# Decays of a gated linear attention: running products by a scan, or sums of logarithms by a triangular matrix product

## The chip, the cores and the metric

The kernel runs on one core of a Trainium2 chip. The metric is the device time of one execution in microseconds (us). The engines of the core are called by the names of the profile: PE (matrix products), DVE (vector), ACT (functions and copies), POOL (general purpose; it also issues the indirect DMAs), and SP (issues the other DMAs).

## What is computed

Three stages in sequence: a gated linear attention, a mixture of experts with one expert per token, and a dense layer with `h*cos(h)`. The change is in the attention alone:

```python
f = 1.0 / (1.0 + np.exp(-f_logit))          # [4, 8, 768, 48]
for t in range(S):
    state = f[:, :, t, :, None] * state + np.einsum('bhd,bhe->bhde', k[:, :, t], v[:, :, t])
    y[:, :, t] = np.einsum('bhd,bhde->bhe', q[:, :, t], state)
```

Its output, 3072 tokens of 384 numbers, goes to the experts (each token to the one with the largest logit) and from there to the last layer.

## The kernel before

**Units.** The attention works on 24 units: 4 sequences, each of 6 chunks of 128 time steps. A unit holds all 8 heads of its chunk, as 4 pairs (`NP`): 48 numbers of head 2p on partitions 0 to 47, of head 2p+1 on partitions 64 to 111, the 128 time steps along the free dimension, so that a gate tile is 128x512. The rows between are padding.

**Gates of a unit u.** `gate_a` (ACT) takes exp(-f_logit), `gate_g` (ACT) adds one: g = 1/f. `gate_b` (DVE) runs four scans, one for each pair, that multiply g along time: r = 1/P, P being the running product of f within the chunk. `gate_ln` and `gate_exp` (ACT) give p0 = exp(-ln r), an approximate P. `gate_k` (POOL) makes k*r, `gate_q` (POOL) makes a = q*p0. `gate_d` (DVE) makes d = r*p0 and the chunk's last product `plast`, and `gate_e` (DVE) makes q = (2-d)*a, a Newton step that takes the error out of p0.

**Products of a unit.** On PE: `scores` (s, 8 products of k and q, L748), `ktrans` (kt, 4 transposes of k, L761), `y_own` (yi, the masked scores by v, L782, after a product with zeros, L777), `y_before` (y, the state of the chunk before, L792), `kvmm` (kv, k by v, L804), `xmm` (x, L830, which puts y in token order and makes the router's logits). DVE masks the scores out of PSUM (`sc`, L754) and updates the state (`S_sb`: L815 adds the product out of PSUM, L816 multiplies by `plast`). ACT copies the other results out of PSUM.

**Beside them**, from about unit 5 on, POOL scatters each unit's tokens to their experts by an indirect DMA (`xs`, L928) and splits the experts' weights in a high and a low part (`wl`, L117). SP loads units, v, weights, and clears `xs`.

**Order.** Each engine takes its instructions in program order. The class `Plan` writes that order: each step has an engine, a duration, a due time and a list of steps that it needs; `T` is the time from one unit's due times to the next one's. `keep_warm` puts small products of ones on PE where the plan has a gap there. The inputs lie in rings of five (`NIN`), and a load waits until the unit five before has given its buffer back.

Of the kernel before, what the change touches and what calls it, by code (L numbers as in the profile page):

```python
# [6 lines left out]
F32 = mybir.dt.float32  # L7
# [16 lines left out]
UB = S // CH  # L24
NP = H // 2
# [7 lines left out]
RMAX = 2.0 ** 62  # L33
F64_LO = 1.0 / 2 ** 15 * 1.125
# [606 lines left out]
def attention(tc, A, c):  # L641
    nc = tc.nc
    pe, dve, act, pool, sp = nc.tensor, nc.vector, nc.scalar, nc.gpsimd, nc.sync
    W = c["W"]
    xs, ident, ones, zeros, ctab, acc, plast = (c[n] for n in ("xs", "ident", "ones", "zeros", "ctab", "acc", "plast"))
    with ExitStack() as ctx:
        lc = ctx.enter_context(tc.tile_pool(name="lc", bufs=1))
        mask = lc.tile([128, 128], F32, name="mask")
        ucst = lc.tile([128, 128], F32, name="ucst")
        wcat = lc.tile([128, NP, 112], F32, name="wcat")  # L650
        urank = lc.tile([128, 128], BF16, name="urank")
        smask = lc.tile([128, E, GMAX], F32, name="smask")
# [3 lines left out]
        rmax = lc.tile([128, CH], F32, name="rmax")  # L656
        inp = ctx.enter_context(tc.tile_pool(name="inp", bufs=2))
        gat = ctx.enter_context(tc.tile_pool(name="gat", bufs=2))
# [9 lines left out]
        qkf = [inp.tile([128, 3, NP, CH], F32, name=f"qkf{i}", bufs=1) for i in range(NIN)]  # L668
        units, vs = {}, {}

        def load(u, apart=False):
            t = qkf[u % NIN]
            for n in ((slice(0, 1), slice(1, 3)) if apart else (slice(0, 3),)):
                for j in range(2):
                    sp.dma_start(out=t[j * 64:j * 64 + D, n], in_=A["qkf"][u, j][:, n])
            units[u] = dict(f=t[:, 0], k=t[:, 1], q=t[:, 2])
# [6 lines left out]
        st = {}  # L683
        P = Plan()
# [7 lines left out]
        def gate_a(u):  # L692
            tl = units.pop(u)
            st[u] = dict(g=gat.tile([128, NP, CH], F32, name="g"), tl=tl)
            act.activation(out=st[u]["g"], in_=tl["f"], func=AF.Exp, scale=-1.0)

        def gate_g(u):
            g = st[u]["g"]
            act.activation(out=g, in_=g, func=AF.Copy, bias=1.0)

        def gate_b(u):
            s = st[u]
            r = gat.tile([128, NP, CH], F32, name="r", bufs=3)
# [149 lines left out]
        def route(gi):  # L853
# [31 lines left out]
            ps = ps_r.tile([128, E, n], F32, name="rps", tag="ps")  # L885
# [137 lines left out]
        T = 5.8  # L1023
        for u in range(NU):
            b, ch = T * u, u % UB
            if u >= NIN:
                P.add(("ld", u), "sp", 1.65, load, (u,), b - 14, [("a", u - NIN), ("k", u - NIN)])
            if u >= 3:
                P.add(("ldv", u), "sp", 0.6, load_v, (u,), b, [("kv", u - 5), ("yi", u - 5)])
            P.add(("e", u), "act", 0.52, gate_a, (u,), b - 7.6, [("ld", u), ("b", u - 2)])  # L1030
            P.add(("g", u), "act", 0.52, gate_g, (u,), b - 7.0, [("e", u)])
            P.add(("b", u), "dve", 1.4, gate_b, (u,), b - 6.0, [("g", u), ("d", u - 3), ("k", u - 3), ("ln", u - 3)])
            P.add(("ln", u), "act", 0.52, gate_ln, (u,), b - 4.6, [("b", u), ("a", u - 2), ("d", u - 2)])
            P.add(("ex", u), "act", 0.52, gate_exp, (u,), b - 4.0, [("ln", u)])
            if u:
                P.add(("k", u), "pool", 1.23, gate_k, (u,), b - 3.5, [("b", u), ("s", u - 3), ("kt", u - 3)])
            else:
                P.add(("k", u), "dve", 0.6, gate_k, (u, dve), b - 3.5, [("b", u)])
            if u:
                P.add(("a", u), "pool", 1.23, gate_q, (u,), b - 2.4, [("ex", u), ("y", u - 3)])  # L1040
            else:
                P.add(("a", u), "dve", 0.6, gate_q, (u, dve), b - 2.4, [("ex", u)])
            P.add(("d", u), "dve", 0.8, gate_d, (u,), b - 1.8, [("ex", u), ("q", u - 2)])
            P.add(("q", u), "dve", 0.62, gate_e, (u,), b - 0.9, [("d", u), ("a", u)])
            P.add(("s", u), "pe", 1.2, scores, (u,), b, [("q", u), ("k", u), ("v0", u - 1), ("v1", u - 2)])
# [8 lines left out]
            P.add(("st", u), "dve", 0.65 if ch < UB - 1 else 0.0, state, (u,), b + T + 5.9, [("kv", u), ("y", u - 1), ("d", u)])  # L1054
# [41 lines left out]
        P.issue({("ldc", 0): 17.6} | {("ld", i): t for i, t in enumerate((4.0, 7.6, 11.0, 14.4, 16.6))}  # L1096
# [48 lines left out]
def layouts(inputs):  # L1145
    import numpy as np
    a = {}
    t = np.stack([inputs[n] for n in ("f_logit", "k", "q")]).reshape(3, B, NP, 2, UB, CH, D)
    a["qkf"] = np.ascontiguousarray(t.transpose(1, 4, 3, 6, 0, 2, 5)).reshape(NU, 2, D, 3, NP, CH)
    v = inputs["v"].reshape(B, H, UB, CH, D).transpose(0, 2, 3, 1, 4).reshape(NU, CH, DM)  # L1150
# [18 lines left out]
    a["pad"] = np.zeros((16, 3, NP, CH), np.float32)  # L1169
    a["pad"][:, 0] = 30.0  # L1170
# [16 lines left out]
_IN = ("qkf", "v", "wcat", "wgate", "cst", "pad", "itab", "ctab", "slots", "wmoe", "wffn")  # L1187
# [16 lines left out]
```

## Time and profile before

| what | value |
|---|---|
| runs of the kernel | 926.71, 928.77, 918.55 us; median 926.71 |
| the profiled execution | 921.53 us, span of its instructions 919.7 us |
| granted clock of PE, mean | 0.948 |
| PE busy over the span | 832.2 us (90%) |
| DVE busy over the span | 733.6 us (80%) |
| ACT busy over the span | 386.8 us (42%) |
| POOL busy over the span | 413.7 us (45%) |

The profiled execution lies within the runs. Shares of the whole span are a mean over the three stages; the attention has to be read by itself, and the rows below do that.

### The profile page before, as it was taken

The numbers are of one execution on the slowest core, as the hardware profiler recorded it, in microseconds if no ns is written. First come the engines' busy times: TensorE is split into PE (matmuls) and PEld (weight loads), VectorE is DVE, ScalarE is ACT, GpSimd is POOL, SyncE is SP. The second block draws the span as 40 slices with busy tenths as digits, with TensorE's granted clock in tenths as the row PEclk, the third lists the DMA queues.
The fourth block names the chain that finished last, engine by engine and source line by source line (L and its number), as shares of the span: only waits on it lengthen the run. The fifth ranks groups of instructions, "written<-read, shape, count | busy, mean of one in ns | idle before, by whom it ended". The sixth has DMA issues, their size and how long they took to land.

```text
span 919.7 us, 14462 instructions
## 1 busy us (share of the span) xinstructions
PE 832.2 (90%) x5253; PEld 740.9 (81%) x5253; DVE 733.6 (80%) x1288; ACT 386.8 (42%) x740; POOL 413.7 (45%) x369
## 2 busy tenths in 40 slices
PE   6887677789899898898899999999999999999995
PEld 5766566677788797797799898989999999999885
DVE  6999999886797796886876887778777777787990
ACT  3674566435343343353344444333333333333440
POOL 3546575643122222221225476544644554545652
PEclk7898899798899898999989999999999999999998
DMA  9995646203675855955846200000000000000001
GB/s 185 294 308 155 172 122 174 96 28 99 163 177 174 213 130 192 222 131 199 215 145 145 36 18 1 32 4 1 35 1 0 35 1 1 35 1 1 35 1 38
DMA packets 42033, 92.26 MB, mean 100 GB/s; under 512 B 12576, under 2 KB 19872, under 8 KB 41952
## 3 DMA queue, kind: packets, MB, share of 16 engines
q1 hardware_dynamic: 38880, 81.79, 34.0%
q0 software_dynamic: 3072, 9.45, 2.8%
q8 instruction: 43, 0.70, 0.3%
q14 instruction: 38, 0.31, 0.1%
HBM read 69.93 MB, written 21.29 MB: 99 GB/s over the span
## 4 chain that ended last, share of the span: by engine, by line
PE 58%; DVE 25%; DMA 9%; issue 4%; ACT 1%; POOL 1%; SPq 1%; DVEq 0%; POOLq 0%; ACTq 0%
PE ps L622 9%; PE ps L623 9%; PE ps L625 9%; PE o L374 6%; PE o L372 6%; PE o L373 6%; DMA xe<-xs 5%; DVE r L705 4%; PE o L201 3%; PE o L202 3%; PE o L203 3%; DVE S_sb L816 3%; DVE sc L754 2%; DVE a L738 2%; DVE d L731 2%
## 5 line engine op out<-in xcount | busy, mean ns | idle before, releaser
L368 POOL TENSOR_TENSOR lo<-r,hi 128x512 fp32r<-128x512 f32 (+1 forms) x96 | 148.1, 1543 | 172.4 <-ACT hi L367 91.5
L117 POOL TENSOR_TENSOR wl<-ws,wh 128x384 fp32r<-128x384 f32 x96 | 101.3, 1055 | 220.7 <-ACT wh L113 164.8
L622 PE MATMUL ps<-yh,wh 128*128 128x512 f32 (+1 forms) x480 | 189.2, 394 | 0.2 <-ACT yh L614 0.2
L623 PE MATMUL ps<-yh,wl 128*128 128x512 f32 (+1 forms) x480 | 187.3, 390 | 0.0
L625 PE MATMUL ps<-yl,wh 128*128 128x512 f32 (+1 forms) x480 | 135.0, 390 | 0.0
L367 ACT CAST hi<-r 128x512 fp32r<-128x512 f32 (+1 forms) x96 | 56.2, 586 | 168.7 <-DVE r L362 167.8
L630 DVE TENSOR_SCALAR n<-ps 128x512 f32<-128x512 f32 x96 | 66.2, 690 | 68.6 <-PE ps L625 68.6
L374 PE MATMUL o<-wh,lo 128*128 128x384 f32 x352 | 119.0, 338 | 1.3 <-POOL lo L368 1.3
L372 PE MATMUL o<-wl,hi 128*128 128x384 f32 x352 | 118.6, 337 | 0.0
L373 PE MATMUL o<-wh,hi 128*128 128x384 f32 x352 | 118.3, 336 | 0.0
L625 PEld LDWEIGHTS ps<-yl,wh 128*128 128x128 f32 x480 | 92.9, 194 | 16.1
L622 PEld LDWEIGHTS ps<-yh,wh 128*128 128x128 f32 x480 | 93.1, 194 | 11.8 <-ACT yh L614 0.3
L623 PEld LDWEIGHTS ps<-yh,wl 128*128 128x128 f32 x480 | 92.7, 193 | 11.3
L638 ACT ACTIVATE r<-r,quarter 128x512 f32<-128x512 f32 x96 | 69.6, 724 | 73.8 <-DVE r L637 73.8
L189 ACT ACTIVATE hi<-ps 128x448 fp32r<-128x448 f32 x64 | 34.9, 545 | 101.5 <-PE ps L625 98.9
L113 ACT CAST wh<-ws 128x384 fp32r<-128x384 f32 x160 | 74.8, 508 | 4.5 <-DMA ws<-in_wmoe 4.5
L637 DVE SCALAR_TENSOR_TENSOR r<-n,r 128x512 f32<-128x512 f32 x96 | 70.1, 730 | 3.3
L201 PE MATMUL o<-hi,wh 128*128 128x448 f32 x192 | 71.9, 374 | 0.0
L202 PE MATMUL o<-hi,wl 128*128 128x448 f32 x192 | 71.5, 373 | 0.0
L203 PE MATMUL o<-lo,wh 128*128 128x448 f32 x192 | 71.2, 371 | 0.0
L373 PEld LDWEIGHTS o<-wh,hi 128*128 128x128 f32 x352 | 66.1, 188 | 4.3
L372 PEld LDWEIGHTS o<-wl,hi 128*128 128x128 f32 x352 | 66.2, 188 | 3.9
(152 smaller groups left out, 1582.2 us busy)
## 6 DMA issues: line engine op xcount, KB each, us to landing
ws<-in_wmoe SPq DMA_DIRECT2D x64, 384.0 KB, 5.9
qkf<-in_qkf SPq DMA_DIRECT2D x46, 288.0 KB, 6.4
cs<-in_wffn SPq DMA_DIRECT2D x24, 512.0 KB, 6.9
wffn<-ca SPq DMA_DIRECT2D x24, 256.0 KB, 5.2
ws<-wffn SPq DMA_DIRECT2D x16, 384.0 KB, 3.9
xs<-xe SPq DMA_DIRECT2D x7, 770.0 KB, 10.2
v<-in_v SPq DMA_DIRECT2D x24, 200.0 KB, 4.8
xe<-xs SPq DMA_DIRECT2D x28, 168.4 KB, 8.4
```

Source lines behind the costliest of these rows:

```text
L113: self.nc.scalar.copy(out=h, in_=w)
L117: (eng or self.nc.gpsimd).tensor_tensor(out=l, in0=w, in1=h.bitcast(F32), op=ALU.subtract)
L201: pe.matmul(yps[e][d], wh[:, cs], hi, start=m == 0, stop=False)
L202: pe.matmul(yps[e][d], wl[:, cs], hi, start=False, stop=False)
L203: pe.matmul(yps[e][d], wh[:, cs], lo, start=False, stop=m == FT - 1)
L368: pool.tensor_tensor(out=los, in0=r[:, cs], in1=his.bitcast(F32), op=ALU.subtract)
L372: pe.matmul(o, hi, wl[:, cs], start=m == 0, stop=False)
L373: pe.matmul(o, hi, wh[:, cs], start=False, stop=False)
L374: pe.matmul(o, lo, wh[:, cs], start=False, stop=m == NF - 1)
L622: nc.tensor.matmul(out, wh[:, ws[d]], xh[:, d, :], start=d == 0, stop=False)
L623: nc.tensor.matmul(out, wl[:, ws[d]], xh[:, d, :], start=False, stop=False)
L625: nc.tensor.matmul(out, wh[:, ws[d]], xl[:, d, :], start=False, stop=d == 2)
```

## The change

The logits of f come a second time, in token order: a new input `ft`, 128 time steps on the partitions and 384 numbers along the free dimension. For each unit DVE clamps them from below (`gate_f`), ACT makes exp(-f_logit) and ln(1 + that) (`gate_e`, `gate_ln`), which is -ln f, into a tile padded to 64 columns a head (`sps`), and PE multiplies it by the triangle of ones (`gate_c`, four products of 128x128 by 128x128): the sum over the steps so far, already with head and number on the partitions and time along the free dimension. ACT then reads that PSUM tile twice, exp of it (r) and exp of its negative (p). DVE makes k = min(r, 2^62)*k in one instruction, POOL makes q = q*p, DVE copies `plast` from p. The scans, the ln and exp of r, d and the Newton step are gone, and k is no longer POOL's.

```diff
-        ps_kv = ctx.enter_context(tc.tile_pool(name="ps_kv", bufs=1, space=PSUM))
+        ps_c = ctx.enter_context(tc.tile_pool(name="ps_c", bufs=1, space=PSUM))
...
-        ps_r = ctx.enter_context(tc.tile_pool(name="ps_r", bufs=1, space=PSUM))
+        kr = ctx.enter_context(tc.tile_pool(name="ps_kr", bufs=1, space=PSUM)).tile([128, 512], F32, name="kr")
...
+        def load_f(u):
+            fs[u] = inp.tile([128, DM], F32, name="f", bufs=NIN)
+            sp.dma_start(out=fs[u], in_=A["ft"][u])
...
-            for p in range(NP):
-                dve.tensor_tensor_scan(out=r[:, p, :], data0=s["g"][:, p, :], data1=rmax, initial=1.0,
-                                       op0=ALU.mult, op1=ALU.min)
...
+        def gate_f(u):
+            dve.tensor_scalar(out=fs[u], in0=fs[u], scalar1=FMIN, scalar2=None, op0=ALU.max)
+
+        def gate_e(u):
+            st[u] = {}
+            act.activation(out=fs[u], in_=fs[u], func=AF.Exp, scale=-1.0)
+
+        def gate_ln(u):
+            act.activation(out=sps[u % 2][:, :, 0:D], in_=fs.pop(u).rearrange("t (h d) -> t h d", d=D), func=AF.Ln, bias=one)
+
+        def gate_c(u):
+            ps = st[u]["c_ps"] = ps_c.tile([128, NP, CH], F32, name="cps", tag="ps")
+            keep_warm(ps)
             for p in range(NP):
+                pe.matmul(ps[:, p, :], sps[u % 2][:, 2 * p:2 * p + 2, :].rearrange("t h d -> t (h d)"), mask,
+                          start=True, stop=True)
+
+        def gate_r(u):
...
+            act.activation(out=s["r"], in_=s["c_ps"], func=AF.Exp)
+
+        def gate_p(u):
...
+            act.activation(out=s["p"], in_=s["c_ps"], func=AF.Exp, scale=-1.0)
...
-            eng.tensor_tensor(out=s["k"], in0=s["tl"]["k"], in1=s["r"], op=ALU.mult)
+            dve.scalar_tensor_tensor(out=s["k"], in0=s["r"], scalar=RMAX, in1=kq[u % NIN][:, 0], op0=ALU.min, op1=ALU.mult)
...
-            dve.tensor_tensor(out=d, in0=s["r"], in1=s["p0"], op=ALU.mult)
-            dve.scalar_tensor_tensor(out=plast[:, u, :], in0=d[:, :, CH - 1], scalar=2.0, in1=s["p0"][:, :, CH - 1],
-                                     op0=ALU.subtract, op1=ALU.mult, reverse0=True)
...
-            dve.scalar_tensor_tensor(out=s["q"], in0=s.pop("d"), scalar=2.0, in1=s["a"],
-                                     op0=ALU.subtract, op1=ALU.mult, reverse0=True)
+        def gate_last(u):
+            dve.tensor_copy(out=plast[:, u, :], in_=st[u]["p"][:, :, CH - 1])
...
-        T = 5.8
+        T = 6.5
...
+                P.add(("ldf", u), "sp", 0.6, load_f, (u,), b - 15, [("ln", u - NIN)])
+                P.add(("ld", u), "sp", 1.2, load, (u,), b - 14, [("a", u - NIN), ("k", u - NIN)])
...
+            P.add(("f", u), "dve", 0.3, gate_f, (u,), b - 9.0, [("ldf", u)])
+            P.add(("e", u), "act", 0.5, gate_e, (u,), b - 8.4, [("f", u)])
+            P.add(("ln", u), "act", 0.5, gate_ln, (u,), b - 7.8, [("e", u), ("c", u - 2)])
+            P.add(("c", u), "pe", 1.15, gate_c, (u,), b - 7.0, [("ln", u), ("r", u - 1), ("p", u - 1)])
```

The k and q halves of a unit are loaded by two DMAs of 48 rows each as before, now without f (`kq`), and f by one DMA of 128 rows. The results of `kvmm` and of the router's counts share one PSUM tile, `kr`. The rest of the attention and all of the two later stages are the same code.

In DVE's program a unit in the middle of the attention (it multiplies the state, so it isn't the first of a sequence) stands as follows. Before, with d, a, r and g as above and `lg` the router's logits:

```order
L731 TENSOR_TENSOR d<-r,p_961 128x512
L732 SCALAR_TENSOR_TENSOR plast<-d,p_961 128x4
L705 SCALAR_TENSOR_TENSOR r<-g,rmax 128x128 x4
L754 TENSOR_TENSOR sc<-sps,mask 128x512 x2
L738 SCALAR_TENSOR_TENSOR a<-d,a 128x512
L815 TENSOR_TENSOR S_sb_95<-S_sb_94,kvps 128x192
L816 TENSOR_TENSOR S_sb_95<-S_sb_95,plast 128x192
L850 TENSOR_REDUCE lg<-xps 128x16
```

And now, with f the clamp of a unit that lies five or six units ahead of the k beside it:

```order
L700 TENSOR_SCALAR f<-f 128x384
L813 TENSOR_TENSOR S_sb_95<-S_sb_94,kr 128x192
L814 TENSOR_TENSOR S_sb_95<-S_sb_95,plast 128x192
L700 TENSOR_SCALAR f<-f 128x384
L729 SCALAR_TENSOR_TENSOR k<-r,kq_130 128x512
L752 TENSOR_TENSOR sc<-sps,mask 128x512 x2
L848 TENSOR_REDUCE lg<-xps 128x16
L737 COPY plast<-p 128x4
```

Four scans, d and the Newton step have left, k and the clamp have come; the clamp is the one row there that needs a DMA's data.

On POOL the same stretch before, with a scatter (`xs`) and the weight parts (`wl`) among the gates' products:

```order
L928 DMA xs<-x,idx 6656x385
L117 TENSOR_TENSOR wl<-ws,wh 128x384
L721 TENSOR_TENSOR k<-qkf_127,r 128x512
L117 TENSOR_TENSOR wl<-ws,wh 128x384
L928 DMA xs<-x,idx 6656x385
L844 COPY x<-itab 128x1
L726 TENSOR_TENSOR a<-qkf_127,p_1058 128x512
```

And now:

```order
L118 TENSOR_TENSOR wl<-ws,wh 128x384
L926 DMA xs<-x,idx 6656x385
L118 TENSOR_TENSOR wl<-ws,wh 128x384
L734 TENSOR_TENSOR a<-kq_134,p 128x512
L842 COPY x<-itab 128x1
L118 TENSOR_TENSOR wl<-ws,wh 128x384
L926 DMA xs<-x,idx 6656x385 x2
```

The k rows are gone, and each unit has one product less between scatters and weight parts.

## Rows read from the trace of the kernel before

**Rows 1.** Windows: length, busy PE, PEld, DVE, ACT, POOL; PEclk, DMA share, GB/s.

```profile
0.00:22.00 22.00, 14.32 (x149) 12.53 (x151) 15.03 (x30) 8.43 (x13) 9.17 (x15) 0.76 0.90 185
22.00:61.00 39.00, 34.86 (x429) 28.87 (x429) 35.81 (x85) 25.08 (x49) 17.38 (x21) 0.92 1.01 305
61.00:203.00 142.00, 105.01 (x1264) 87.15 (x1266) 134.16 (x272) 76.70 (x158) 88.94 (x88) 0.90 0.51 134
```

**Rows 2.** Scores on PE, and the experts' first product: timeline (start, us; idle before).

```profile
21.81 2.08 PE L748 MATMUL sps<-a,k 64*128 64x128 f32 x16 [2.02 <-DVE a L738]
...
61.28 1.16 PE L748 MATMUL sps<-a,k 64*128 64x128 f32 x16 [0.47 <-DVE a L738]
...
195.59 1.92 PE L748 MATMUL sps<-a,k 64*128 64x128 f32 x16 [4.51 <-DVE a L738]
...
202.82 1.16 PE L748 MATMUL sps<-a,k 64*128 64x128 f32 x16
...
221.98 0.48 PE L622 MATMUL ps<-yh,wh 128*128 128x448 f32 x1 [0.19 <-ACT yh L614]
```

**Rows 3.** DVE's groups from 61 to 203 us (busy, mean ns, idle before).

```profile
L705 DVE TENSOR_TENSOR_SCAN r<-g,rmax 128x128 f32<-128x128 f32 x60 | 32.3, 597 | 0.0
L816 DVE TENSOR_TENSOR S_sb<-S_sb,plast 128x192 f32<-128x192 f32 x11 | 21.0, 1907 | 0.4
...
L738 DVE SCALAR_TENSOR_TENSOR a<-d,a 128x512 f32<-128x512 f32 x17 | 17.2, 1014 | 1.9 <-POOL a L726 1.9
L731 DVE TENSOR_TENSOR d<-r,p 128x512 f32<-128x512 f32 x16 | 13.5, 841 | 0.0
L732 DVE SCALAR_TENSOR_TENSOR plast<-d,p 128x4 f32<-128x4 f32 x16 | 9.0, 560 | 0.6
```

**Rows 4.** Timeline of DVE: the state's product twice, k of unit 0.

```profile
6.86 0.69 DVE L721 TENSOR_TENSOR k<-qkf,r 128x512 f32<-128x512 f32 x1
...
183.67 0.36 DVE L816 TENSOR_TENSOR S_sb<-S_sb,plast 128x192 f32<-128x192 f32 x1
...
189.81 5.13 DVE L816 TENSOR_TENSOR S_sb<-S_sb,plast 128x192 f32<-128x192 f32 x1
```

**Rows 5.** Timeline of POOL beside the second of them, first and last of six rows.

```profile
188.92 1.28 POOL L928 DMA_INDIRECT xs<-x,idx  x1 [0.17 <-POOL a L726]
...
193.73 0.98 POOL L117 TENSOR_TENSOR wl<-ws,wh 128x384 fp32r<-128x384 f32 x1
```

**Rows 6.** POOL's k from 61 to 203 us, by groups.

```profile
L721 POOL TENSOR_TENSOR k<-qkf,r 128x512 f32<-128x512 f32 x16 | 22.1, 1379 | 8.9 <-issue 3.9 <-DVE r L705 3.8 <-PE ktps L761 1.1
```

**Rows 7.** Who waited for whom from 61 to 203 us: total, times, longest.

```profile
PE sps L748 <- DVE a L738: 13.9, 9, 4.5
...
PE yps L792 <- DVE S_sb L816: 11.9, 7, 6.1
```

**Rows 8.** Timeline of PE over one unit's products without a wait.

```profile
40.30 1.15 PE L830 MATMUL xps<-wcat,y 128*128 128x112 f32 x8
41.28 0.38 PE L777 MATMUL yps<-ones,zeros 128*128 128x512 bf16 x1
41.59 1.09 PE L782 MATMUL yps<-sc,v 128*64 128x128 f32 x16
42.62 1.16 PE L748 MATMUL sps<-a,k 64*128 64x128 f32 x16
43.71 1.09 PE L792 MATMUL yps<-a,S_sb 64*64 64x128 f32 x16
44.73 0.67 PE L804 MATMUL kvps<-v,kt 128*64 128x48 f32 x16
45.33 0.66 PE L761 MATMUL ktps<-ident,k 128*128 128x128 f32 x4
```

**Rows 9.** DMA issues from 20 to 60 us (KB each, median us to landing).

```profile
qkf<-in_qkf SPq DMA_DIRECT2D x16, 288.0 KB, 10.1
```

**Rows 10.** A tensor_scalar of DVE within SBUF, experts' last layer, 500 to 560 us.

```profile
L631 DVE TENSOR_SCALAR n<-n x14: 426/796/1219, 510.6 to 558.9; 128x512 f32<-128x512 f32 x14
```

More of the change, by code (lines that the diff above doesn't have):

```diff
@@ L33 @@
 RMAX = 2.0 ** 62
+FMIN = -40.0
 F64_LO = 1.0 / 2 ** 15 * 1.125
@@ L655, in attention @@
         S_sb = [lc.tile([128, NP * D + 16], F32, name=f"S_sb{i}") for i in range(2)]
-        rmax = lc.tile([128, CH], F32, name="rmax")
+        one = lc.tile([128, 1], F32, name="one")
+        sps = [lc.tile([128, H, 64], F32, name=f"soft{i}") for i in range(2)]
         inp = ctx.enter_context(tc.tile_pool(name="inp", bufs=2))
@@ L663, in attention @@
         ps_y = ctx.enter_context(tc.tile_pool(name="ps_y", bufs=1, space=PSUM))
-        ps_kv = ctx.enter_context(tc.tile_pool(name="ps_kv", bufs=1, space=PSUM))
+        ps_c = ctx.enter_context(tc.tile_pool(name="ps_c", bufs=1, space=PSUM))
         ps_x = ctx.enter_context(tc.tile_pool(name="ps_x", bufs=1, space=PSUM))
-        ps_r = ctx.enter_context(tc.tile_pool(name="ps_r", bufs=1, space=PSUM))
-        qkf = [inp.tile([128, 3, NP, CH], F32, name=f"qkf{i}", bufs=1) for i in range(NIN)]
-        units, vs = {}, {}
+        kr = ctx.enter_context(tc.tile_pool(name="ps_kr", bufs=1, space=PSUM)).tile([128, 512], F32, name="kr")
+        kq = [inp.tile([128, 2, NP, CH], F32, name=f"kq{i}", bufs=1) for i in range(NIN)]
+        fs, vs = {}, {}
         def load(u, apart=False):
-            t = qkf[u % NIN]
-            for n in ((slice(0, 1), slice(1, 3)) if apart else (slice(0, 3),)):
+            t = kq[u % NIN]
+            for n in ((slice(0, 1), slice(1, 2)) if apart else (slice(0, 2),)):
                 for j in range(2):
-                    sp.dma_start(out=t[j * 64:j * 64 + D, n], in_=A["qkf"][u, j][:, n])
-            units[u] = dict(f=t[:, 0], k=t[:, 1], q=t[:, 2])
+                    sp.dma_start(out=t[j * 64:j * 64 + D, n], in_=A["qkf"][u, j][:, 1:3][:, n])
+        def load_f(u):
+            fs[u] = inp.tile([128, DM], F32, name="f", bufs=NIN)
+            sp.dma_start(out=fs[u], in_=A["ft"][u])
         def load_v(u):
@@ new lines, in gate_ln @@
+        def gate_ln(u):
[3 more added lines that the diff above has]
+            keep_warm(ps)
+            for p in range(NP):
+                pe.matmul(ps[:, p, :], sps[u % 2][:, 2 * p:2 * p + 2, :].rearrange("t h d -> t (h d)"), mask,
+                          start=True, stop=True)
+        def gate_r(u):
+            s = st[u]
+            s["r"] = gat.tile([128, NP, CH], F32, name="r")
+            act.activation(out=s["r"], in_=s["c_ps"], func=AF.Exp)
@@ L735, in gate_e @@
-        def gate_e(u):
-            s = st[u]
-            s["q"] = s["a"]
-            dve.scalar_tensor_tensor(out=s["q"], in0=s.pop("d"), scalar=2.0, in1=s["a"],
-                                     op0=ALU.subtract, op1=ALU.mult, reverse0=True)
+            s["q"] = gat.tile([128, NP, CH], F32, name="a", bufs=3)
+            eng.tensor_tensor(out=s["q"], in0=kq[u % NIN][:, 1], in1=s["p"], op=ALU.mult)
+        def gate_last(u):
+            dve.tensor_copy(out=plast[:, u, :], in_=st[u]["p"][:, :, CH - 1])
@@ L983, in attention @@
         pool.memset(zeros, 0.0)
+        dve.memset(one, 1.0)
+        for t in sps:
+            dve.memset(t, 0.0)
         for i in range(NIN):
+            load_f(i)
+            if i == 0:
+                sp.dma_start(out=mask, in_=A["cst"][:, 128:256])
             for lo, eng in ((32, dve), (96, pool)):
                 if i < 2:
-                    eng.memset(qkf[i][lo:lo + 32, 0], 30.0)
-                    eng.memset(qkf[i][lo:lo + 32, 1:3], 0.0)
+                    eng.memset(kq[i][lo:lo + 32], 0.0)
                 else:
-                    sp.dma_start(out=qkf[i][lo + 16:lo + 32], in_=A["pad"])
+                    sp.dma_start(out=kq[i][lo + 16:lo + 32], in_=A["pad"])
             load(i, i == 0)
@@ L1031, in attention @@
[L1031 to L1045, printed above, removed]
+            P.add(("f", u), "dve", 0.3, gate_f, (u,), b - 9.0, [("ldf", u)])
@@ L1046, in attention @@
+            P.add(("a", u), "pool" if u else "dve", 1.28 if u else 0.68, gate_q, (u,) if u else (u, dve), b - 3.0,
+                  [("p", u), ("ld", u), ("y", u - 3)])
+            P.add(("pl", u), "dve", 0.1, gate_last, (u,), b - 2.0, [("p", u)])
+            P.add(("s", u), "pe", 1.2, scores, (u,), b, [("a", u), ("k", u), ("v0", u - 1), ("v1", u - 2)])
             P.add(("v0", u), "dve", 0.62, scores_evac, (u, 0), b + 1.2, [("s", u), ("y", u - 2)])
@@ L1053, in attention @@
             P.add(("kv", u), "pe", 0.6 if ch < UB - 1 else 0.0, kvmm, (u,), b + T + 5.2, [("kte", u), ("st", u - 1), ("ldv", u)])
-            P.add(("st", u), "dve", 0.65 if ch < UB - 1 else 0.0, state, (u,), b + T + 5.9, [("kv", u), ("y", u - 1), ("d", u)])
+            P.add(("st", u), "dve", 0.65 if ch < UB - 1 else 0.0, state, (u,), b + T + 5.9, [("kv", u), ("y", u - 1), ("pl", u)])
             P.add(("x", u), "pe", 1.1, xmm, (u,), b + 2 * T + 1.7, [("ye", u), ("xe", u - 1), ("lg", u - 1)])
@@ L1095, in attention @@
         keep_warm(ps_x.tile([128, NP, 112], F32, name="xps", tag="ps"), 65)
-        P.issue({("ldc", 0): 17.6} | {("ld", i): t for i, t in enumerate((4.0, 7.6, 11.0, 14.4, 16.6))}
+        P.issue({("ldc", 0): 17.6} | {("ld", i): t for i, t in enumerate((5.0, 7.6, 11.0, 14.4, 16.6))}
+                | {("ldf", i): t for i, t in enumerate((2.5, 6.0, 9.5, 13.0, 15.5))}
                 | {("ldv", i): t for i, t in enumerate((8.6, 12.2, 17.1))}, {"sp": 17.2, "pe": 6.9})
@@ L1149, in layouts @@
     a["qkf"] = np.ascontiguousarray(t.transpose(1, 4, 3, 6, 0, 2, 5)).reshape(NU, 2, D, 3, NP, CH)
+    f = inputs["f_logit"].reshape(B, H, UB, CH, D).transpose(0, 2, 3, 1, 4)
+    a["ft"] = np.ascontiguousarray(f).reshape(NU, CH, DM)
     v = inputs["v"].reshape(B, H, UB, CH, D).transpose(0, 2, 3, 1, 4).reshape(NU, CH, DM)
```

40 lines of the change are left out of this document (9 added, 31 removed).

## Prediction

> **What bounds the kernel now.** I read the windows by stage first. From 61 to 203 us, where scatters and weight splits run beside the gates, DVE is busy 134.16 of 142 us, PE 105.01, POOL 88.94, ACT 76.70 [rows 1]: DVE is full and the others wait. From 22 to 61 us the DMAs are full (share 1.01, 305 GB/s) and DVE and PE are both near 90% [rows 1]. The scores on PE give the pace. Scores 1 start at 21.81, scores 7 at 61.28, scores 23 at 202.82 us [rows 2]: 6.58 us a unit early, (202.82 - 61.28)/16 = 8.85 us later. The experts start at 221.98 us, 19.2 us after the last scores [rows 2]. That tail, and everything after it, is the same code, so the change is worth what it takes from scores 23.
>
> The table of waits names whom PE waits for later: DVE's q for the scores, 13.9 us, and the state for y, 11.9 us [rows 7].
>
> Why is DVE full? Its groups there [rows 3] are partly work and partly waiting inside the instruction. The state's product took 0.36 us at 183.67 but 5.13 us at 189.81 [rows 4]. In that stretch POOL ran six instructions without a break, from 188.92 to 194.71 us [rows 5], and DVE's instruction ended just after them. The mean of that group is 1907 ns [rows 3], so it waits 11 x (1.91 - 0.36) = 17 us. Scans, d, `plast` and the Newton step stand in the same way. Before, DVE and POOL between them have more work that excludes the other than the stretch has room for.
>
> On the wait of one DVE instruction behind POOL, the Trainium skill, page SBUF — State Buffer, section "SBUF: two separate sides", says that the two engines share a port pair as "an exclusive lock, not a bandwidth split", held for the whole instruction. The trace agrees that DVE is stopped outright, but shows more than the rule: DVE didn't get in between POOL's instructions, it waited through the rest of one and five more. By the rule alone the longest wait would be one POOL instruction, 1.28 us, the state's group would cost at most 0.36 + 1.28 = 1.64 us each, and DVE's sum below would fall by 0.2 us a unit; the forecast would stay.
>
> **The change, part by part, for the stretch from 61 to 203 us (16 units).**
>
> *DVE, removed.* The four groups scan 32.3, Newton step 17.2, d 13.5 and `plast` 9.0 us [rows 3] make 72.0 of the 134.2 us busy. Left are 62.2 us, 3.9 us a unit, the state's waits included.
>
> *DVE, added.* k costs 0.69 us where POOL was idle (unit 0) [rows 4]; the Newton step, also two inputs in SBUF, took 1.01 with its waits [rows 3]. The clamp: a tensor_scalar of 512 columns within SBUF took 426 ns at its shortest and 796 in the middle [rows 10], by 384/512 0.32 to 0.60 us. The copy of `plast` is between nothing and the 0.56 us of the old step [rows 3]. Together 1.0 to 2.2 us; I take 1.6, the middle, since POOL stays busy. DVE then needs 3.9 + 1.6 = 5.5 us a unit (4.9 to 6.1).
>
> *POOL.* k goes, 22.1 of 88.94 us [rows 1, 6]: 66.8 us, 4.2 us a unit. The runs of POOL instructions that DVE waits behind get shorter by the k in each.
>
> *ACT.* Four instructions go and four come, two of them over 384 columns in place of 512. ACT was busy 54% [rows 1]; nothing on the path.
>
> *PE, the price.* A unit without waits ran x, zero, yi, s, y and kv from 40.30 to 45.33, 5.03 us, and kt took 0.66 [rows 8]: 5.7 us. One unit in six has no y and zero (1.02 + 0.31 us) and one in six no kv (0.60) [rows 8], so the mean is 5.4. The four new products are bounded below by kt, four transposes of the same size, 0.66 us, and above by x, four f32 products of 112 columns in 0.98 us [rows 8], or 1.12 at 128 columns. They are f32 products as x is: I take 1.12, so 6.5 us a unit on PE (6.0 to 6.5). This is now the longest of the engines, where before it was DVE.
>
> *Waits that stay.* PE waited 13.9 + 11.9 = 25.8 us for DVE [rows 7], 1.6 us a unit, with DVE 94% full. With DVE at 5.5 of some 7 us I take 0.6, bounds 0 and 1.6. A unit then takes 6.5 + 0.6 = 7.1 us (6.5 to 8.1) in place of 8.85.
>
> *The early stretch.* DVE's order has the clamp of unit u as its one row that needs a DMA's data, and it stands five units ahead of k: the clamp of 14 right before k of 9 and the masks of 8. What is queued behind it is the whole of DVE, and PE behind that. By the sizes in SP's new order 17.9 MB are loaded or cleared up to f of unit 14 (15 f of 0.197 MB, 14 k and q of 0.393, ten v of 0.205, seven clears of 0.79, two weight halves of 0.39, 1.1 of pads and tables). The trace moved 22 us x 185 GB/s = 4.1 MB by 22 us and 305 GB/s after it [rows 1]: f of 14 lands at 22 + (17.9 - 4.1)/0.305 = 67 us, and scores 9 follow at about 69. By PE alone, 8 x 6.5 us after 21.81 [rows 2], they would start at 74 if scores 1 stayed where they are; they should come earlier, since the first units no longer wait for k and q before their gates start. I take 71. f as a DMA of its own adds no bytes, and landing took 10.1 us here [rows 9] with five units loaded ahead: cover enough at 6.5 us a unit.
>
> *The sum.* Scores 23 start at 71 + 14 x 7.1 = 170 us in place of 202.82: 32 us less. The ends are 69 + 14 x 6.5 = 160 (43 less) and 74 + 14 x 8.1 = 187 (15 less). Against the profiled execution, 921.53 us, that is 889 (879 to 906). The median of the runs is 5 us above it, so 894 measured from there; I say 891, between the two.
>
> **The rivals.**
>
> *A, the wait moves on.* k and the clamp each wait behind POOL as the state's product does, 1.55 us [rows 3, 4]. DVE needs 3.9 + (0.69 + 1.55) + (0.32 + 1.55) + 0.2 = 8.2 us a unit and stays the bound: 71 + 14 x 8.2 = 186, 905 us. For it: POOL keeps its scatters and weight parts, and the two new rows come after masks out of PSUM, during which POOL gets hold. Against it: POOL has a quarter less to do, and of two waiting rows in succession only the first pays. The Trainium skill, page SBUF — State Buffer, section "Who interferes with whom", has a DVE instruction with two SBUF inputs, which k is, contend with a POOL instruction that reads SBUF: it would give this rival's kind of time.
>
> *B, PE falls to its lower clock, and it gets slower.* After 4.51 us without work the scores at 195.59 took 1.92 us in place of 1.16 [rows 2], at the lower of the clock's two levels (1.2 and 2.4 GHz). The program has 95 of the products of ones that fill gaps, where it had 220. If clamps that wait for DMAs hold DVE, and PE behind it, PE's longer unit runs at half speed in a share x of the units: 6.5 x (1 + x) + 0.6 us. It decides from 71 + 14 P = 203, P = 9.4, x = 0.36; at x = 0.5 scores 23 start at 216 us: 935. Against it: PE would be busy 6.5 of 7.1 us, denser than the 105 of 142 us at which the granted clock was 0.90 [rows 1].
>
> *C, it doesn't do what it says.* The scans were only where DVE happened to wait; POOL's own run (4.2 us a unit plus its waits for scatters and for ACT) and the chain through it keep 8.85 us a unit, and only the start gains: 71 + 14 x 8.85 = 195, 8 us less, 914. Against it: d and the Newton step took 0.84 and 1.01 us on the mean [rows 3] where the like k took 0.69 without a wait [rows 4], so most of what leaves is work.
>
> *D, no waits at all.* PE's floor, scores 1 earlier too: 875 or less.
>
> **How the numbers follow.** Forecast 0.56, A 0.19, C 0.10, D 0.09, B 0.06. A measurement of this kernel, whose runs lie 1.1% apart, can't tell less than 1% from no change: 917 to 936 from the median. Faster is the forecast, A, D and 0.03 of C, which lies at the edge: 0.87; the same is the rest of C and 0.01 of B: 0.08; slower is the rest of B: 0.05. The range takes in the bounds and A: 876 to 911, and leaves out D, B and most of C.
>
> **What would show it.** Right: in the changed profile DVE falls to about 5.5 of 7 us a unit, PE is the fullest engine in the middle of the attention at a clock near 1, scores follow each other by about 7.1 us, and the last start near 170 us; the four new products take 1.12 us together. Wrong: the state's product and k at 1.5 us and more on the mean (A), a granted clock below 0.85 there (B), the old step of 8.85 us (C), or DVE standing idle before the clamp with a DMA as the releaser for more than some 4 us in total, in which case scores 9 come well after 74 us.

## The result, and the profile after

The changed kernel takes 896.7 us (median of four runs, 892.5 to 899.3) where the kernel before took 926.6 beside it: ratio 0.969 (0.962 to 0.976), 30 us less. The forecast was 891 us, from 876 to 911. The profiled execution after took 899.3 us with a span of 897.4, so that of after is the slowest of its four, while that of before lies 5 us under its median: from profile to profile only 22 us can be found.

The windows by stage of the changed kernel (columns as in [rows 1]; 174 is where scores 23 start, 196.8 the experts):

```profile
0.00:22.00 22.00, 16.67 (x190) 15.29 (x191) 9.33 (x21) 9.82 (x17) 5.16 (x11) 0.92 0.82 192
22.00:61.00 39.00, 35.82 (x425) 29.78 (x426) 20.54 (x62) 22.16 (x46) 10.08 (x16) 0.96 1.00 317
61.00:174.00 113.00, 106.35 (x1282) 88.97 (x1280) 74.95 (x193) 72.38 (x151) 61.79 (x70) 0.95 0.60 165
174.00:196.80 22.80, 19.50 (x178) 16.46 (x178) 12.09 (x69) 10.15 (x23) 4.89 (x9) 0.85 0.20 66
196.80:897.40 700.60, 662.19 (x3253) 597.99 (x3253) 539.86 (x849) 269.41 (x506) 294.54 (x238) 0.97 0.30 79
```

The third row answers to the third of [rows 1]: 113 us in place of 142, and PE, not DVE, is the busy engine, 106 of 113 us (DVE 75) at a granted clock of 0.95. The timeline of PE at six places, first product of the experts last (answers to [rows 2]):

```profile
73.85 1.16 PE L746 MATMUL sps<-a,k 64*128 64x128 f32 x16 [0.49 <-POOL a L734]
...
84.17 2.08 PE L746 MATMUL sps<-a,k 64*128 64x128 f32 x16 [3.48 <-POOL a L734]
...
92.43 1.16 PE L713 MATMUL cps<-mask,soft 128*128 128x128 f32 x8
93.52 1.16 PE L746 MATMUL sps<-a,k 64*128 64x128 f32 x16
...
173.87 1.16 PE L746 MATMUL sps<-a,k 64*128 64x128 f32 x16
...
196.81 0.47 PE L623 MATMUL ps<-yh,wh 128*128 128x448 f32 x1 [0.19 <-ACT yh L615]
```

Scores 9 start at 73.85 and scores 23 at 173.87: (173.87 - 73.85)/14 = 7.14 us a unit. Before, scores 9 stood here (timeline of PE):

```profile
78.84 1.16 PE L748 MATMUL sps<-a,k 64*128 64x128 f32 x16
```

By the same two scores it was 8.86 us a unit. The triangle's products c hold PE for 1.09 us, from 92.43 to 93.52. From scores 23 to the experts it is 22.9 us, where it was 19.2 [rows 2]. DVE's groups from 61 to 174 us (answer to [rows 3]):

```profile
L729 DVE SCALAR_TENSOR_TENSOR k<-r,kq 128x512 f32<-128x512 f32 x16 | 19.0, 1187 | 11.9 <-ACT r L719 10.8 <-DMA ws<-in_wmoe 0.9
L737 DVE COPY plast<-p 128x4 f32<-128x4 f32 x16 | 7.5, 469 | 0.0
L814 DVE TENSOR_TENSOR S_sb<-S_sb,plast 128x192 f32<-128x192 f32 x10 | 4.8, 484 | 0.3
L700 DVE TENSOR_SCALAR f<-f 128x384 f32<-128x384 f32 x11 | 3.9, 353 | 4.5 <-DMA f<-in_ft 4.5
```

Here the state's product is L814: 484 ns in place of 1907. Most of its waiting is gone in this profile; in two later ones of the same kernel (runs 5 and 9 below) it took 617 and 908 ns.

Whom does PE still wait for? The row of PE at 84.17 says POOL's a, 3.48 us, and the scores after it run at the lower clock (2.08 us in place of 1.16). The timeline of POOL just before:

```profile
75.31 1.04 POOL L926 DMA_INDIRECT xs<-x,idx  x1 [0.43 <-DMA xs<-x,idx]
81.46 1.36 POOL L926 DMA_INDIRECT xs<-x,idx  x1 [5.11 <-DMA xs<-x,idx]
82.85 1.27 POOL L734 TENSOR_TENSOR a<-kq,p 128x512 f32<-128x512 f32 x1
```

Two scatters stand in a row in POOL's queue. The second waits for the first to land, 5.11 us without any work, and a, for which the scores wait, stands behind both. This is the kind of row on which the experiments turn.

### The profile page after: what moved, and what is told of

The parts are those of the page before. It is cut to its first block, busy times and chain, and to the rows that moved or that the text cites. A ratio compares the mean times of both kernels' runs of the same rounds, so it can differ in the third digit from the quotient of the medians.

```text
span 897.4 us, 14522 instructions
## 1 busy us (share of the span) xinstructions
PE 840.5 (94%) x5320; PEld 748.5 (83%) x5320; DVE 656.8 (73%) x1191; ACT 383.9 (43%) x740; POOL 376.5 (42%) x344
## 4 chain that ended last, share of the span: by engine, by line
PE 67%; DMA 13%; DVE 9%; issue 4%; POOL 1%; ACT 1%; SPq 1%; POOLq 0%; DVEq 0%; ACTq 0%
PE ps L623 9%; PE ps L624 9%; PE ps L626 9%; PE o L375 7%; PE o L373 6%; PE o L374 6%; DMA xe<-xs 5%; DMA ws<-in_wmoe 4%; PE o L202 3%; PE o L203 3%; PE o L204 3%; PE sps L746 2%; DMA xs<-x,idx 2%; PE xps L828 2%; PE yps L780 2%
```

## The experiments

The theory at the start was the prediction's: DVE was the bound, PE is it now. The rival was C: the scans hid little, and POOL's queue set the pace. Ratios are to the kernel before, run beside each. Runs 1 to 4, 5 to 8 and 9 to 12 shared a chip each, so versions of different groups are best compared by ratio. The expectations call PE TensorE, DVE VectorE, ACT ScalarE and POOL GpSimd. The table puts all profiles side by side; all columns but the last are from the timeline of PE, "the rest" is the span's end less the experts' start.

| kernel | scores 9, us | scores 23, us | us a unit between | to the experts, us | the rest, us | median, us |
|---|---|---|---|---|---|---|
| before | 78.84 | 202.82 | 8.86 | 19.2 | 697.7 | 926.6 |
| changed | 73.85 | 173.87 | 7.14 | 22.9 | 700.6 | 896.7 |
| 1 old, k on DVE | 75.38 | 195.44 | 8.58 | 15.9 | 704.9 | 915.5 |
| 2 old, no scan | 73.40 | 197.71 | 8.88 | 20.0 | 706.0 | 923.8 |
| 3 old, bare | 72.66 | 187.03 | 8.17 | 18.0 | 704.4 | 909.5 |
| 4 changed, c twice | 76.68 | 180.34 | 7.40 | 19.5 | 705.5 | 905.2 |
| 5 changed again | 70.84 | 168.90 | 7.00 | 21.6 | 702.8 | 896.2 |
| 6 scatters apart | 70.54 | 163.81 | 6.66 | 32.3 | 701.2 | 900.9 |
| 7 c in halves | 72.39 | 165.70 | 6.67 | 25.1 | 705.1 | 898.7 |
| 8 changed, k on POOL | 72.40 | 176.88 | 7.46 | 22.6 | 704.3 | 906.2 |
| 9 changed, third time | 73.31 | 174.78 | 7.25 | 22.7 | 703.2 | 899.1 |
| 10 apart early only | 72.75 | 164.70 | 6.57 | 21.4 | 702.9 | 891.4 |
| 11 old, bare, k on DVE | 73.13 | 175.69 | 7.33 | 20.2 | 699.9 | 904.5 |
| 12 changed, a on DVE | 72.14 | 167.30 | 6.80 | 22.3 | 706.5 | 898.5 |

**1. One part alone: k leaves POOL.**

```diff
-P.add(("k", u), "pool", 1.23, gate_k, (u,), b - 3.5, ...
+P.add(("k", u), "dve", 0.7, gate_k, (u, dve), b - 3.5, ...
```

> The kernel before, with one thing of the change alone: k goes from GpSimd to VectorE (same tensor_tensor). Theory (VectorE was full between 61 and 203 us, 134 of 142 us, by work and by waiting behind GpSimd): 16 k of 0.69 us add 11 us there, and the 22 us that leave GpSimd take at most about as much waiting off; so no gain: 920 to 945 us, ratio 0.99 to 1.02. Rival (GpSimd's own run of k, a, scatters and weight parts set the pace, and k leaving it is what the change gained): 8.85 us a unit falls by up to 1.38, some 15 to 22 us faster, 905 to 912.

Measured: 915.5 us, ratio 0.984 (0.979 to 0.990): 14 us faster, nearly the rival. DVE got 16 more instructions and stayed full (115 of the 120 us between scores 9 and 23), yet its state's product, 1907 ns in [rows 3], lost its waits (DVE's groups of this kernel, 61 to 187 us):

```profile
L705 DVE TENSOR_TENSOR_SCAN r<-g,rmax 128x128 f32<-128x128 f32 x62 | 29.6, 538 | 0.0
...
L816 DVE TENSOR_TENSOR S_sb<-S_sb,plast 128x192 f32<-128x192 f32 x10 | 3.6, 358 | 0.3
```

**2. One part alone: the scans' work goes.**

```diff
-for p in range(NP):
-    dve.tensor_tensor_scan(out=r[:, p, :], data0=s["g"][:, p, :], data1=rmax, ...)
+dve.tensor_scalar(out=r, in0=s["g"], scalar1=RMAX, scalar2=None, op0=ALU.min)
```

> The kernel before, with the four scans of a unit replaced by one min over the same 512 columns: the running product is left out (r is the single step's factor), and the overflow guard is set so that it can't fire; all else, the Newton step and k on GpSimd too, is as before. Theory: VectorE loses 32.3 us less 16 passes of about 0.6, 23 us of the 134 between 61 and 203 us, and nothing is added to TensorE, so about 1.4 us a unit: 8.85 becomes 7.4, 895 to 908 us. Rival C (the scans hid nothing): within 1% of before, 917 to 936.

Measured: 923.8 us, ratio 0.993 (0.990 to 0.997). The theory fell here. The windows of this kernel (61 us to scores 23) have DVE at 110 of 137 us, nobody full, and PE's granted clock at 0.85, where it was 0.90:

```profile
61.00:198.00 137.00, 105.30 (x1226) 89.80 (x1231) 109.77 (x222) 74.15 (x152) 81.45 (x86) 0.85 0.52 137
```

and the pace is what it was, 8.88 us a unit. The timeline of POOL, then DVE, then PE of the same kernel at one long unit, a row or two of each, shows why:

```profile
130.49 1.01 POOL L926 DMA_INDIRECT xs<-x,idx  x1 [2.64 <-DMA xs<-x,idx]
131.54 1.27 POOL L724 TENSOR_TENSOR a<-qkf,p 128x512 f32<-128x512 f32 x1
...
132.84 1.74 DVE L736 SCALAR_TENSOR_TENSOR a<-d,a 128x512 f32<-128x512 f32 x1 [3.26 <-POOL a L724]
...
134.64 2.08 PE L746 MATMUL sps<-a,k 64*128 64x128 f32 x16 [2.94 <-DVE a L736]
```

A scatter waits on POOL, a behind it, the Newton step on DVE behind a, the scores on PE behind that. DVE stood idle before its Newton step for 12.9 us, waiting for POOL's a, where it was 1.9 before [rows 3] (DVE's groups of this kernel, 61 to 198 us):

```profile
L736 DVE SCALAR_TENSOR_TENSOR a<-d,a 128x512 f32<-128x512 f32 x16 | 13.5, 845 | 12.9 <-POOL a L724 12.9
```

Part of the time taken off DVE became waiting for POOL.

**3. The removal without its price.**

```diff
-dve.tensor_tensor(out=d, in0=s["r"], in1=s["p0"], op=ALU.mult)
-dve.scalar_tensor_tensor(out=plast[:, u, :], in0=d[:, :, CH - 1], ...)
+dve.tensor_copy(out=plast[:, u, :], in_=s["p0"][:, :, CH - 1])
...
-dve.scalar_tensor_tensor(out=s["q"], in0=s.pop("d"), ...)
```

and the scans replaced as in 2.

> The kernel before without scans (one min in their place), without d and without the Newton step (the last column of p is copied instead): running product and correction are left out, no product with the triangle is put in, k stays on GpSimd; the overflow guard is set so that it can't fire. This is the change's removal without its price. Theory: VectorE loses some 54 of 134 us, TensorE needs 5.4 us a unit and 0.6 of waits, so 6.0 to 6.4 us a unit after 61 us: scores 23 at 157 to 165, 875 to 885 us, that is 12 to 20 us less than the changed kernel, which pays 1.1 us a unit on TensorE for the four products. Rival (GpSimd, which keeps k, is what bounds once the scans are gone): 7 us a unit or more, 893 to 905, no better than the changed kernel.

Measured: 909.5 us, ratio 0.976 (0.971 to 0.982). With nothing added to PE it is not 12 to 20 us faster than the changed kernel but some 6 to 11 slower (ratio 0.976 against 0.965 to 0.970), and slower than the rival's 905 too. Its table of waits (61 to 187 us) names POOL's k:

```profile
PE ktps L754 <- POOL k L719: 11.7, 5, 3.5
```

**4. PE's price doubled.**

```diff
-for p in range(NP):
+for p in list(range(NP)) * 2:
     pe.matmul(ps[:, p, :], sps[u % 2][:, 2 * p:2 * p + 2, :]..., mask, start=True, stop=True)
```

> The changed kernel with the four products of the triangle made twice into the same place (the second overwrites the first). Theory (TensorE is the bound now, 106.4 of 113 us busy): all of it shows, 24 x 1.09 = 26 us, 16 to 26 as far as the early units wait for DMAs: 913 to 923 us. Rival A (VectorE behind GpSimd's lock still sets the pace): TensorE has room, less than 8 us: under 905.

Measured: 905.2 us, ratio 0.972 (0.966 to 0.978), against 896 to 899 and 0.965 to 0.970 for the changed kernel: 6 to 9 of the 26 us by the medians, 2 to 7 by the ratios. That is far from the theory and at the rival's edge. PE is now full, at a clock of 1.00 (windows, 61 us to scores 23), of the long units three late ones of 8.3 to 9.2 us are left, and a full unit takes 7.6 us:

```profile
61.00:180.00 119.00, 116.79 (x1412) 100.33 (x1413) 77.88 (x190) 73.50 (x153) 62.66 (x70) 1.00 0.53 155
```

So the changed kernel's PE has some 0.5 us a unit in it, of waiting and of work at a lower clock (0.95 there), which the second c used up first.

**Revised theory.** PE's own work, near 6.6 us a unit, is one bound; the other is POOL's queue, in which scatters that wait hold a (and before the change k too) back. Run 5 is the changed kernel itself.

> The changed kernel once more, unaltered, beside the next three on the same chip, so that they can be compared with it to less than a per cent: 892 to 902 us.

Measured: 896.2 us, ratio 0.965 (0.960 to 0.969).

**6. The scatters apart.**

```diff
-done[name] = free["sp"] + self.AFTER
+done[name] = free["sp"] + self.AFTER + 2.5
```

> The changed kernel with one constant of the planner altered: a scatter counts as landed 2.5 us later than it did. It changes no instruction, only the order: where GpSimd had two scatters in a row and a behind them, a now stands between them. Theory (revised after the first four runs: GpSimd's queue stands at the second scatter until the first has landed, 3 to 5 us, and a, for which the scores wait, stands behind it; four units of the changed kernel take 8 to 10 us in place of 6.7 for that): these long units vanish, 4 x 2 to 3 us, so 6.6 to 6.9 us a unit in place of 7.14 and 5 to 12 us less in all, 885 to 892. Rival (the long units are TensorE's lower clock or late loads of f): within 3 us of the changed kernel.

Measured: the pace fell as the theory said, to 6.66 us a unit, and scores 23 came 5 us before those of run 5. But the whole took 900.9 us, ratio 0.968 (0.964 to 0.973), 5 us more than run 5 and outside both ranges. The timeline of POOL at the end shows who gave it back:

```profile
175.17 0.98 POOL L926 DMA_INDIRECT xs<-x,idx  x1 [0.45 <-POOL x L842]
...
179.86 0.96 POOL L926 DMA_INDIRECT xs<-x,idx  x1 [0.57 <-POOL idx L905]
183.27 0.96 POOL L926 DMA_INDIRECT xs<-x,idx  x1 [2.45 <-DMA xs<-x,idx]
191.54 0.96 POOL L926 DMA_INDIRECT xs<-x,idx  x1 [7.31 <-DMA xe<-xs]
```

Scatters that had been put off are left over after the last a, at least 3.4 us apart, and the load of the first expert's rows waits for the one at 183.27 (the one at 191.54 in turn for that load): 32.3 us from scores 23 to the experts.

**7. c from fp32r halves.**

```diff
-act.activation(out=sps[u % 2][:, :, 0:D], in_=fs.pop(u)..., func=AF.Ln, bias=one)
+act.activation(out=fs[u], in_=fs[u], func=AF.Ln, bias=one)
+act.copy(out=sph[u % 2][:, :, 0:D], in_=fs[u]...)
+dve.tensor_tensor(out=spl[u % 2][:, :, 0:D], in0=fs.pop(u)..., in1=sph[u % 2]..., op=ALU.subtract)
-pe.matmul(ps[:, p, :], sps..., mask, start=True, stop=True)
+for t in (sph, spl):
+    pe.matmul(ps[:, p, :], t[u % 2]..., maskr, start=t is sph, stop=t is spl)
-T = 6.5
+T = 6.0
```

> The changed kernel with the softplus split into a rounded high part (one more copy on ScalarE) and the rest (one more subtraction on VectorE), both in the fp32r type in which the experts' products run, so that a unit has four products with the high and four with the low part in place of four f32 products that count as eight; the planner's step is 6.0 in place of 6.5. First theory (TensorE is the bound): c falls from 1.09 to about 0.55 us, 0.54 x 24 = 13 us less, 882 to 888. Revised theory (part of TensorE's time is waiting for GpSimd's a anyway; the doubled c cost 0.46 of its 1.09 us a unit): 3 to 8 us less, 888 to 894. Rival (fp32r products of 128 columns are no faster than f32 ones): 8 or more products of the same length, no gain, or slower by VectorE's extra 0.4 us a unit: 896 to 910.

Measured: 898.7 us, ratio 0.966 (0.962 to 0.970), the rival. The timeline of PE has eight products in 1.04 us, up to the 85.27 of the next row:

```profile
84.23 0.33 PE L722 MATMUL cps<-maskr,softh 128*128 128x128 f32 x1
84.40 0.27 PE L722 MATMUL cps<-maskr,softl 128*128 128x128 f32 x1
...
85.07 0.27 PE L722 MATMUL cps<-maskr,softl 128*128 128x128 f32 x1
85.27 0.67 PE L811 MATMUL kr<-v,kt 128*64 128x48 f32 x16
```

c is hardly shorter, so its pace of 6.67 us has probably come from the other order that goes with the step of 6.0; no run tried that order alone.

**8. k back on POOL.**

```diff
-dve.scalar_tensor_tensor(out=s["k"], in0=s["r"], scalar=RMAX, in1=kq[u % NIN][:, 0], ...)
+(pool if u else dve).tensor_tensor(out=s["k"], in0=kq[u % NIN][:, 0], in1=s["r"], op=ALU.mult)
```

> The changed kernel with k back on GpSimd (a plain product: the cap of r is left out). Theory of the prediction (work taken off VectorE was the gain, GpSimd has room at 4.2 + 1.4 = 5.6 us a unit): VectorE is relieved of 0.7 to 1.2 us a unit, TensorE stays the bound, 7.1 to 7.4 us a unit, within 5 us of the changed kernel, up to 902. Rival, as the run without scans and correction suggests (TensorE waited 24 us for GpSimd's k there, at 8.1 us a unit): 8.1 us a unit or more, 15 to 25 us slower, 910 to 922.

Measured: 906.2 us, ratio 0.975 (0.970 to 0.980) against run 5's 0.965: 10 us slower, 7.46 us a unit, between the two. PE's waits for POOL's a (61 us to scores 23) are 6.9 us where run 5 had 2.5, none is for k.

> The changed kernel again, unaltered, beside the next three on the same chip: 893 to 900 us.

Measured: 899.1 us, ratio 0.970 (0.966 to 0.973).

**10. Apart, but not at the end.**

```diff
-done[name] = free["sp"] + self.AFTER
+done[name] = free["sp"] + self.AFTER + 2.5 * (name[1] < 12)
```

> The changed kernel with the planner's 2.5 us on a scatter's landing for the first 12 units alone; from unit 12 on the constant is the old one. With it for all units, scores followed each other by 6.66 us, scores 23 came 5 us earlier, but the last four scatters stood in a row at the end, each waiting for the one before to land, and the experts started 32.3 us after scores 23 in place of 21.6. Theory: the pace stays 6.6 to 6.8 us a unit and the tail goes back to 21 to 24 us: experts at 186 to 189, 3 to 7 us less than the changed kernel. Rival (the scatters need the time wherever they stand, so that what the pace gains the end gives back): within 2 us of it.

Measured: 891.4 us, ratio 0.960 (0.957 to 0.963), clear of run 9 beside it: 7.7 us less, the fastest version here. The experts start at 186.11. The timeline of POOL now has an a between the scatters:

```profile
75.84 1.02 POOL L926 DMA_INDIRECT xs<-x,idx  x1 [0.46 <-DMA ws<-in_wmoe]
...
80.72 1.27 POOL L734 TENSOR_TENSOR a<-kq,p 128x512 f32<-128x512 f32 x1 [0.43 <-ACT p L724]
82.15 1.28 POOL L926 DMA_INDIRECT xs<-x,idx  x1 [0.16 <-issue]
```

and the windows have PE at 101.3 of 104 us, at a clock of 1.00, with no wait for a left in the table:

```profile
61.00:165.00 104.00, 101.27 (x1274) 84.88 (x1274) 73.37 (x194) 71.28 (x151) 63.10 (x70) 1.00 0.63 178
```

**11. The removal without its price, k on DVE too** (the edits of 1 and 3 together).

> The kernel before without scans (one min in their place), without d and the Newton step, and now with k on VectorE too: GpSimd carries what it carries in the changed kernel, VectorE about the same, and TensorE has no products with the triangle. The running product and the correction are left out, and the overflow guard is set so that it can't fire. Theory (the gain is k off GpSimd and work off VectorE together, the price is c on TensorE): TensorE needs 5.6 us a unit, and with the scatters in GpSimd's queue as they are some 0.5 to 1 us of waits: 6.1 to 6.6 after the loads are in, 880 to 890 us, 6 to 16 less than the changed kernel. Rival (the queue of scatters on GpSimd bounds at about 7.1 whatever TensorE does, c is hidden): within 5 us of the changed kernel, 891 to 901.

Measured: 904.5 us, ratio 0.977 (0.972 to 0.981): by ratio no faster than run 3, slower than the changed kernel by 5 us, and outside both ranges, though PE has no c. PE was busy 102 of the 115 us up to scores 23, and its longest waits, 6.7 us in four, are for POOL's a. But this PE isn't free of the price either. With a step of 5.8 the planner sees gaps on PE and fills them with products of ones, 13.6 us between scores 9 and 23, most of them before the scores (PE's groups of this kernel there):

```profile
L689 PE MATMUL sps<-ones 128*128 128x112 bf16 x150 | 9.8, 223 | 0.0
```

The changed kernel has none there, and 15.1 us of c. So this run doesn't test what c costs. Its profile is also the fastest of its four executions (897.6 us).

**12. a on DVE as well.**

```diff
-P.add(("a", u), "pool" if u else "dve", 1.28 if u else 0.68, gate_q, (u,) if u else (u, dve), b - 3.0,
+P.add(("a", u), "dve", 0.68, gate_q, (u, dve), b - 3.0,
```

> The changed kernel with a on VectorE as well: no step of the gates is left on GpSimd, which keeps scatters, weight parts and ids. Theory (scores wait for a behind scatters in GpSimd's queue): those waits vanish, VectorE gets 0.7 to 0.9 us a unit more (75 of 113 us becomes 87 to 90) and stays below TensorE's 6.65 us a unit, scores 23 at 163 to 166 with the scatters' order at the end little changed, 3 to 8 us less than the changed kernel. Rival (VectorE, with a behind clamps, masks and the routing's small steps that wait behind GpSimd, becomes late, as in the run with k alone moved): 7.4 us a unit or more, slower than the changed kernel by 3 us or more.

Measured: 898.5 us, ratio 0.969 (0.965 to 0.973), the same as run 9. In the profile the attention went as the theory said (6.80 us a unit, the experts 8 us before run 9's), but the rest took 706.5 us, the longest of all. That one profile doesn't show why; it stays open.

## Why the prediction was right, and where it wasn't

**The number is better than the sum.** From profile to profile 32 us were forecast and 22 came. The pace was right, but scores 23 started 4 us later than the 170 of the sum, the tail was 3.8 us longer, and the rest 2.9. That 891 lies within 6 us of the median is in part luck: the profile before, from which the sum starts, was 5 us under its median, and that of after was the slowest of its four.

**PE's 6.5 and the waits' 0.6 were right in size.** Between scores 9 and 23, 14 units, the windows of run 10 and of the changed kernel are:

```profile
72.75:164.70 91.95, 89.80 (x1132) 75.21 (x1131) 63.21 (x177) 61.93 (x131) 54.76 (x61) 1.00 0.58 167
73.85:173.87 100.02, 94.45 (x1131) 79.03 (x1132) 64.75 (x180) 62.30 (x130) 54.97 (x63) 0.95 0.56 156
```

PE's work is 6.4 us a unit at a clock of 1.00. The changed kernel's three profiles (runs 5 and 9 are the other two) are 6.1 to 9.5 us longer than run 10 there: 3.4 to 5.7 us of that is PE standing idle, and 1.8 to 4.7 us the same products at a lower clock (0.95 to 0.98). c took 1.09 against 1.12.

**The waits are for two engines, not one.** The prediction kept a part of PE's waits for DVE [rows 7]. From 61 us to scores 23 PE waited 4.4 us for POOL's a and 2.1 for DVE in the first profile of the changed kernel, 2.5 and 4.1 in run 5, and 1.5 and 5.6 in run 9 (its table of waits):

```profile
PE kr L885 <- DVE oh L873: 2.3, 2, 2.0
PE kr L884 <- DVE S_sb L816: 1.8, 1, 1.8
PE kr L802 <- DVE t L899: 1.5, 1, 1.5
PE sps L746 <- POOL a L734: 1.5, 2, 1.2
```

Behind the 2.0 us for `oh` stands a small DVE instruction of the router that took 3.18 us at 135.61, while POOL ran six instructions without a break from 134.41 to 138.85 (timeline of DVE, then of PE, run 9):

```profile
135.61 3.18 DVE L870 TENSOR_TENSOR d<-lg,mx 128x32 f32<-128x32 f32 x1
...
139.53 0.18 PE L885 MATMUL kr<-oh,urank 128*128 128x32 bf16 x1 [2.01 <-DVE oh L873]
```

So what the prediction had, DVE held up beside POOL, is still there, and a behind scatters comes beside it. With the scatters set apart none is left for a, and 2.0 us for DVE (run 10). That constant also moved weight parts, some loads and clamps, and a few of PE's products, so the 8 us are shown for the order as a whole. Before the change the same queue stood in part one step further back: [rows 7] names DVE's a, and DVE waited 1.9 us before it for POOL's a [rows 3], 12.9 once the scans were gone (run 2). A wait's releaser has a releaser of its own.

**"DVE is full and the others wait" failed as an account of the gain.** The step from 72 us of DVE's work removed to 32 us off scores 23 isn't supported: the scans, 32.3 us of that [rows 3], gave 5 us alone, with a min of 8.2 us in their place (run 2), while k off POOL, which only adds to DVE, gave 14 (run 1), and without either scans or Newton step it was 20 (run 3). Rival C was right about the scans. The parts don't add up: without scans and Newton step it is 20 us with k on POOL and 24 with k on DVE, by ratio the same. The reading that fits, and that no run isolates, is the prediction's own sentence on two engines whose work excludes the other's: relief of either frees in part the same time, and POOL's queue stands between them and the scores. The Trainium skill, page SBUF — State Buffer, section "Who interferes with whom", has a DVE instruction with two SBUF inputs contend with a POOL instruction that reads SBUF; run 1, where k's 22 us off POOL took the state's product from 1907 to 358 ns, bears it out.

**The price was counted in full, and is mostly hidden.** c twice cost 2 to 9 us of 26 (run 4); that is the only run that shows it, since run 11 has products of ones in the place of c. With the scatters out of the way PE is full, and c should be in the pace; no run took c out there.

**DVE** was busy 74.95/16 = 4.7 us a unit in the first profile, under the 4.9 to 6.1: the added k, clamp and copy took 2.0 against 1.6, within bounds, but the 3.9 that was left included waits of the state that vanished. Between scores 9 and 23 it was 4.6 us there but 5.5 and 5.2 in runs 5 and 9 of the same kernel, as forecast. Rival A, that k and clamp take those waits over, holds for k in part (1187 ns, 1623 in run 5, 764 in run 9, against 0.69 us alone) and not for the clamp (353 ns). Rival B came in small, the 1.8 to 4.7 us at a lower clock.

**The early stretch** came out: scores 9 at 70.8 to 73.9 in three profiles, 71 predicted. The DMAs were full there (share 1.00), and f of unit 14 was in at 65.4 to 68.7 us (clamp's starts, after a wait for its DMA), 67 predicted; scores 9 followed by 5 to 6 us in place of 2. One of the prediction's signs of being wrong came up in two of the three profiles: DVE stood idle 4.5 and 4.8 us before clamps after 61 us (3.0 in run 9), but scores 9 were not late by it.

**"That tail is the same code" was wrong by 3.8 us.** The planner's order put one x, one yi with its zeros and one kt behind scores 23 that stood ahead of them before, and left out some products of ones: 2.1 us (the last x starts 9.9 after scores 23, at 183.77 by the timeline, in place of 7.8). The other 1.6 us are late loads and products after it. The rest after the experts' start lies between 697.7 and 706.5 us over all profiles without any change to its code; before's is the shortest. Differences of a few us between single profiles say little for that reason.

**Open.** The changed kernel beats run 11 by some 5 us of the medians, with intervals that just touch. Between scores 9 and 23 PE is equally busy in both (92.7 us in run 11, 91.6 to 94.5), and in the profiles the experts start at 195.9 in run 11 and at 190.5 to 197.5, so no profile shows where the 5 us are. What is left between them is the gates' steps on ACT, f as a load of its own, the products of ones, and the planner's step, 6.5 in place of 5.8. None of them was tried alone.

## What to carry to other kernels

Before counting the gain of work taken off a full engine, follow what that engine's last instruction waits for: if it is a queue that stands still at a DMA's landing, the work removed turns into waiting. In an in-order queue, look at what stands behind an instruction that waits for an earlier transfer; an order that sets such instructions apart was worth 8 us and no work. When a kernel with a part left out is to show that part's price, look at what its planner puts in the gap (run 11). When an order is made by a planner, its last rows are part of the change, and an improvement in the middle must be checked at the end (run 6).

## What the hardware showed that was not expected

A product in fp32r with 128 moving columns took as long a step as half of an f32 one: eight in 1.04 us, against four f32 ones in 1.09. Split in two, nothing is won at this width.

A scatter of 128 rows to the same tensor as the one before waited up to 5.1 us for that one to land (at 81.46 in the changed kernel), and at the end of the attention, where the DMA share is 0.18, it started 3.4 us after the one before (run 6, at 183.27). The Trainium skill, page DMA: Bandwidth & Descriptors, section "Anatomy of one DMA — SWDGE (gpsimd) path", fits 2.0 us plus the bytes over 436 GB/s, an estimate of 2.5 us for these 197 KB. The chain of waits of the changed kernel shows 2.75 for the last one, near it:

```profile
184.19 2.75 DMA xs<-x,idx
```
